# Weight decoding through a ring of three zeroed tiles, scaled copies that GpSimd may take, and an earlier start, in a bucketed attention with a feed-forward layer

## The chip, the cores and the metric

The kernel runs on one core of one Trainium2 chip. The metric is the device time of one execution in microseconds (us), as the median of the runs; lower is better.

## What is computed

The reference has two parts. The first is attention over 4 batches, 8 heads, 768 positions and 64 elements per head, in which a query sees only the keys of its own bucket (the signs of six projections). The second is a feed-forward layer on the attention's output, 3072 tokens by 512.

```python
q_bits = (np.einsum('bhsd,dk->bhsk', q, proj) > 0).astype(np.int64)
k_bits = (np.einsum('bhsd,dk->bhsk', k, proj) > 0).astype(np.int64)
...
mask = q_bucket[:, :, :, None] == k_bucket[:, :, None, :]
scores = scale * np.matmul(q, k.transpose(0, 1, 3, 2))
scores = np.where(mask, scores, -1000000000.0)
...
attn = np.exp(scores - max); attn = attn / (sum + 1e-09); x = attn @ v
h = x @ w_in
g = np.where(h > 0.0, h, alpha * (np.exp(np.minimum(h, 0.0)) - 1.0))
return (g @ w_out).astype(np.float32)
```

q, k, v and proj are float32; w_in (512 x 2048) and w_out (2048 x 512) arrive as float64.

## The kernel before

**Tiling.** Attention runs over 32 pairs of heads: 8 chunks (one batch and one half of its rows) of 4 pairs each. A pair has 6 row tiles of 128 queries, so there are 192 score tiles, numbered G = 0 to 191 (`pair_ops`). A float32 factor enters a matmul as two float16 halves, a high half (a scaled copy, written by `times`) and a low half (what the copy left over, written by `left_over`), and a product is three matmuls. For one score tile TensorE makes the scores (L896), VectorE takes them out of PSUM with the row maximum (L919) and makes the bias (`nb`, L936), ScalarE does the exponential (L947), VectorE the inverse sum (L985, L986), ScalarE or VectorE the high half (`hl`, through `times`, L356 or L358), VectorE the low half (L361), and a transposing DMA turns both for the product with V (L1076). The first four pairs (`whole`) skip the halves: TensorE turns their float32 tiles (`flip`, L963) and multiplies in float32 (L1046).

**Feed-forward.** `moe_ops` follows one chunk behind: matmuls into `h` (L1138), exponential and relu on ScalarE (L1162, L1166), their minimum on VectorE (L1169), two halves again (L356, L361), matmuls into `o` (L1190).

**Weights.** `weight_ops` loads 32 blocks of 128 x 512 float64 as pairs of 16-bit and 32-bit words, in staging places (`U`, three deep, and `raw`). For each block GpSimd zeroes the destination in `W` (L471, `zero`; from the fourth block on behind a one-element copy `tick`, L470, that makes GpSimd wait for an earlier block), ScalarE writes the top 16 bits of every element into it (L474, `top_`), and VectorE joins the low bits (L477, `join`). TensorE sums squares for a bound on all blocks (L489). After that `split` makes two float16 halves of each block in place of the float32 block in front of it: the high half by `hi` (operation `w{i}hi`, ScalarE or VectorE, L356 or L358), the low half by `lo` on VectorE (L361). Block i + 1 can be split only when block i has been, since its halves overwrite what block i was read from. `v_splits` makes the halves of V (`v{b}{p}hi` and `lo`), one operation of 128 x 768 per pair and batch.

**Order.** All operations are entered in a plan (`Plan.add`) with the engines that may run them ("AV" is ScalarE or VectorE), a cost, a due time and the operations they wait for. `Plan.order` then fixes the order on each engine: the first engine named takes the operation unless it would be busy for long and another is free earlier (`YIELD`). The instructions are issued in that order, engine by engine, and on the chip each engine works through its own list. SyncE (`S`) issues nearly all DMAs in one such list. In the first 32 us TensorE fills its gaps with `spin` matmuls (L1283) whose result nobody reads.

**Start.** `prep_ops` loads K and Q of a pair, scales them, makes halves, and turns them by transposing DMAs (`k_tr` L693, `q_tr` L724); K is duplicated (`k_dup`, L696), and bucket bits are computed from the turned tiles (`bits_ops`: matmuls L755, tests L763 or L776, and copies by DMA L785). `begin_ops` makes constants: GpSimd memsets, and the projection's halves (`rest_`, L412 to L419, all on VectorE). `v_ops` loads V (L803) and squares it on ScalarE (L352).

Of the kernel before, what the change touches and what calls it, by code (L numbers as in the profile page):

```python
# [7 lines left out]
F16 = mybir.dt.float16  # L8
# [20 lines left out]
DIRECT = 1  # L29
# [7 lines left out]
VD = -22  # L37
# [157 lines left out]

TINY = 160.0
# [3 lines left out]
def lsh_attention_moe(  # L200
# [38 lines left out]
    xp = ctx.enter_context(tc.tile_pool(name="xp", bufs=2))  # L239
# [9 lines left out]
        for name, cap in (  # L249
# [30 lines left out]

    ones = const.tile([P, P], BF16, name="ones")
# [14 lines left out]
    eye = W[:, NSI + 1, :P]  # L296
    area["ot"] = [W[:, NSI, :], W[:, NSI + NSO + 1, :]]
# [29 lines left out]
    def sum_over(mx, n):  # L327

        t = ps_a.tile([P, 512], F32, tag="av", name="sum")[:, :n]
        nc.tensor.matmul(t, ones, mx.bitcast(BF16).rearrange("p (n t) -> p n t", t=2)[:, :, 1], start=True, stop=True)  # L330
        return t
# [32 lines left out]
    def begin_ops():  # L364
# [35 lines left out]
        a = add("V", top_, TINY, -40, [loaded], name="pjx")  # L400
# [5 lines left out]
        b = add("P", sum_, 60.0, -40, [a, filled], new=[av], name="pjsum")  # L406

        def rest_():
            _, sc = exponents(pj["t"], 1, 2.0**-17, 13, "pj", small)
            hl = const.tile([P, 2, NB], F16, name="pjhl")  # L410
            pf, z = pj["f"], pj["z"]
            nc.vector.tensor_scalar(hl[:, 0], pf, sc, None, ALU.mult)  # L412
            nc.vector.scalar_tensor_tensor(hl[:, 1], pf, sc, hl[:, 0], ALU.mult, ALU.subtract)
            for n, (at, parts) in enumerate(
                ((1, ((0, P, 0),)), (1, ((0, P, 1),)), (0, ((0, D, 0), (D, P, 1))), (0, ((0, D, 1),)))
            ):
                for a_, z_, x in parts:
# [14 lines left out]
    def weight_ops():  # L432
# [887 lines left out]
```

## Time and profile before

| | |
|---|---|
| median of 3 runs | 858.01 us (857.25 to 860.03) |
| the profiled execution | 857.3 us, span 855.5 us from first to last instruction |
| TensorE busy | 816.5 us (95%), of it 21.9 us spin matmuls |
| ScalarE busy | 704.0 us (82%) |
| VectorE busy | 681.5 us (80%) |
| GpSimd busy | 22.9 us (3%), 15.9 us of it 32 memsets of weight blocks |

The profile names the engines PE (TensorE), DVE (VectorE), ACT (ScalarE), POOL (GpSimd) and SP (SyncE); PEld is TensorE's weight load. Busy shares over the whole span mix three stages: a start, a stretch in which scores of the first chunks and the weights' preparation lie together, and the long rest in which attention of one chunk and the feed-forward layer of the one before run side by side. A tile's name stands without its number, and `out<-in` is what an instruction writes and reads.

### The profile page before, as it was taken

How to read it: one execution, taken by the hardware profiler on the slowest of the kernel's cores; microseconds unless marked ns; L12 is line 12 of the kernel's file. 1: busy time of each engine (PE TensorE's matmuls, PEld its weight loads, DVE VectorE, ACT ScalarE, POOL GpSimd, SP SyncE). 2: the span in 40 equal slices, each digit the busy share in tenths (PEclk: the TensorE clock that was granted, in tenths of full speed). 3: DMA queues.
4: the chain of work that ended last, by engine and by line, in shares of the span. 5: the costliest groups of instructions: out<-in, count | busy, mean ns of one | idle time of the engine just before them, and what ended most of it. 6: DMA issues, size and time to landing. Idle time of an engine off the chain costs nothing. (4 is left out here: it accounts for less than half of the span.)

```text
span 855.5 us, 14970 instructions
## 1 busy us (share of the span) xinstructions
PE 816.5 (95%) x5298; PEld 439.5 (51%) x5301; DVE 681.5 (80%) x1520; ACT 704.0 (82%) x1292; POOL 22.9 (3%) x68
## 2 busy tenths in 40 slices
PE   8889869989999999999999999999999999999997
PEld 3455534444555555545555555555455555555553
DVE  6958999999998877888988778989888777773232
ACT  6679999999978889898888789888888878783543
POOL 3024000000000000000000000000000000000000
PEclk9989999999999999999999999999999999999999
DMA  9788767888989789958977888968877758571101
GB/s 283 141 237 288 267 128 127 150 190 146 152 165 178 126 179 224 183 111 152 181 147 135 138 190 187 216 98 157 167 143 140 131 105 158 98 105 38 38 1 37
DMA packets 367466, 128.99 MB, mean 151 GB/s; under 512 B 342248, under 2 KB 360352, under 8 KB 367392
## 3 DMA queue, kind: packets, MB, share of 16 engines
q1 hardware_dynamic: 367088, 127.91, 73.2%
q8 instruction: 41, 0.67, 0.3%
q14 instruction: 33, 0.27, 0.1%
q10 hardware_dynamic: 304, 0.13, 0.1%
HBM read 35.65 MB, written 6.29 MB: 49 GB/s over the span
## 5 line engine op out<-in xcount | busy, mean ns | idle before, releaser
L1138 PE MATMUL h<-x,W 128*128 128x384 f16 x1536 | 313.2, 327 | 7.8 <-ACT U L1166 7.2
L1190 PE MATMUL o<-W,U 128*128 128x512 f16 x1152 | 307.0, 379 | 2.4 <-ACT U L356 1.8
L947 ACT ACTIVATE pt<-pt,nb,sg 128x768 f32<-128x768 f32 x192 | 196.1, 1022 | 42.9 <-DVE nb L936 42.3
L1138 PEld LDWEIGHTS <-W 128*128 128x128 f16 x1536 | 148.8, 98 | 146.4 <-issue 15.5
L919 DVE TENSOR_SCALAR_CACHE_REDUCE pt<-s 128x768 f32<-128x768 f32 x180 | 171.5, 953 | 17.1 <-PE s L896 16.3
L361 DVE SCALAR_TENSOR_TENSOR hl<-pt,r,hl 128x768 f16<-128x768 f32 x168 | 165.1, 1013 | 7.9 <-ACT hl L356 7.4
L1190 PEld LDWEIGHTS <-U 128*128 128x128 f16 x1152 | 110.0, 97 | 105.6 <-issue 3.5
L896 PE MATMUL s<-K,O 128*128 128x384 f16 x720 | 147.8, 327 | 5.9 <-DVE pt L919 5.1
L356 ACT ACTIVATE hl<-pt,r 128x768 f16<-128x768 f32 x167 | 148.2, 929 | 1.8 <-DMA PT<-hl 0.6
L1169 DVE SCALAR_TENSOR_TENSOR U<-U 128x384 f32<-128x384 f32 x128 | 70.8, 553 | 52.5 <-ACT U L1166 52.2
L896 PEld LDWEIGHTS <-O 128*128 128x128 f16 (+1 forms) x768 | 73.2, 98 | 64.2 <-issue 19.6
L1162 ACT ACTIVATE U<-h,ch 128x384 f32<-128x384 f32 x128 | 73.1, 571 | 36.7 <-PE h L1138 36.5
L356 ACT ACTIVATE U<-U,sgg 128x384 f16<-128x384 f32 x128 | 78.1, 610 | 25.9 <-DVE U L1169 25.9
L361 DVE SCALAR_TENSOR_TENSOR U<-U,sgg 128x384 f16<-128x384 f32 x128 | 78.5, 614 | 22.2 <-ACT U L356 20.0
L1076 PE MATMUL av<-PT,vhl 128*64 128x384 f16 x1008 | 88.9, 327 | 3.1 <-DMA PT<-hl 3.1
L1076 PEld LDWEIGHTS <-vhl 128*64 128x64 f16 x1008 | 57.7, 110 | 33.3 <-issue 12.1
L1166 ACT ACTIVATE U<-h,ch 128x384 f32<-128x384 f32 x128 | 73.0, 571 | 0.0
L985 DVE TENSOR_SCALAR r<-sm 128x2 f32<-128x2 f32 x84 | 13.9, 165 | 31.4 <-ACT pt L947 30.9
L947 ACT ACTIVATION_READ_ACCUMULATOR pt<-pt,nb,sg 128x1 f32 x192 | 37.0, 193 | 0.0
L963 PE MATMUL flip<-W,pt 128*128 128x128 f32 x144 | 23.1, 286 | 3.8 <-ACT PT L356 2.7
L936 DVE TENSOR_SCALAR nb<-m,sg 128x2 f32<-128x2 f32 x96 | 23.4, 244 | 3.1
L1283 PE MATMUL spin<-ones 128*128 128x512 bf16 x81 | 21.9, 414 | 2.1 <-POOL ones L367 2.0
(126 smaller groups left out, 582.8 us busy)
## 6 DMA issues: line engine op xcount, KB each, us to landing
U<-in_moe_w_in_dram SPq DMA_DIRECT2D x12, 512.0 KB
vf<-in_v_dram SPq DMA_DIRECT2D x16, 384.0 KB
U<-in_moe_w_out_dram SPq DMA_DIRECT2D x12, 512.0 KB
qst<-in_q_dram SPq DMA_DIRECT2D x30, 192.0 KB
kst<-in_k_dram SPq DMA_DIRECT2D x14, 384.0 KB
out_dram<-W SPq DMA_DIRECT2D x16, 256.0 KB
PT<-hl SPq DMA_TRANSPOSE x168
W<-in_moe_w_in_dram SPq DMA_DIRECT2D x4, 512.0 KB
```

The source lines that it names most:

```text
L356: nc.scalar.activation(o, x, AF.Copy, scale=s)
L361: nc.vector.scalar_tensor_tensor(o, x, s, hi, ALU.mult, ALU.subtract)
L896: nc.tensor.matmul(s.t[:, y, :HALF], O[x][:rows, j * HC + t, :], K[x][:rows, j * NC + y * HC : j * NC + (y + 1) * HC, :].rearrange("p a b ...
L919: nc.vector.tensor_scalar(pt.t.rearrange("p (n e) -> p n e", n=2), s.t[:, :, :HALF], CLAMP, None, ALU.max, ALU.max, accum_out=m.t[:, y : y ...
L936: nc.vector.tensor_scalar(nb.t, m.t, sg_of(n), -1.0, ALU.mult, ALU.mult)
L947: nc.scalar.activation(pt_.t, pt_.t, AF.Exp, bias=nb.t[:, y : y + 1], scale=sg_of(n), accum_out=sm.t[:, z : z + 1])
L1076: nc.tensor.matmul(av.t[j * D : (j + 1) * D], vs["hl"][p].t[:, j, c, vx, :], PTs[j].t[:, :, px, c, :], start=y == 0, stop=y == 3 * NC - 1,)
L1138: nc.tensor.matmul(h.t, WH[:, g * KT + t, wx, fc * P : (fc + 1) * P], xbuf[NP * ci + t].t[:, xx, :], start=t == 0 and y == 0, stop=t == KT ...
L1162: nc.scalar.activation(e.t, h.t, AF.Exp, scale=c["ch"])
L1166: nc.scalar.activation(hp.t, h.t, AF.Relu, scale=c["ch"])
L1169: nc.vector.scalar_tensor_tensor(e.t, e.t, -1.0, hp.t, ALU.add, ALU.min)
L1190: nc.tensor.matmul(banks[t][:, :DO], g16.t[:, gx, t * P : (t + 1) * P], WH[:, NSI + 1 + f, wx, :], start=f == 0 and y == 0, stop=f == NF - ...
```

## The change

1. **Ring of zeroed tiles.** The 32 memsets of weight blocks and the 15 `tick` copies go. A tile `X` of 8 slots of 128 x 384 float32 takes the place of the pool `xp` (the attention's output halves); its upper four slots serve as three tiles of 128 x 512 (`tops`) that GpSimd zeroes once. ScalarE writes a block's top bits into one of the three (`top_`), and VectorE joins low bits and that tile into `W`. The outputs of later pairs wait for all joins before they use those slots (`topped`).
2. **GpSimd for scaled copies.** `w{i}hi` and `v{b}{p}hi` may run on "GAV", GpSimd first, at a planning cost of 0.9 n + 200 ns (`third`).
3. **The first pair is turned by TensorE.** K and Q of pair 0 go through 24 matmuls of 128 columns against a float16 unit matrix (`turned`) into score banks, and four copies of 128 x 768 bring them to SBUF; the two transposing DMAs of that pair go.
4. **Order.** V's first loads are due earlier (`VD` from -22 to -40), the projection's constants too; the copies of the projection's halves move from VectorE (10 instructions) to ScalarE (6); a sum of the first pairs uses another PSUM bank.

```diff
-VD = -22
+VD = -40
+GP = 0.9
+WH_ = ("GAV", "GAV")
...
+def third(n):
+    return (GP * n + 200.0, *either(n, pointer=True))
...
+    X = const.tile([P, 2 * NP, HALF], F32, name="X")
+    tops = X[:, NP:].rearrange("p a b -> p (a b)").rearrange("p (a b) -> p a b", b=SL)
...
-            nc.vector.tensor_scalar(o, x, s, None, ALU.mult)
+            (nc.gpsimd if e == "G" else nc.vector).tensor_scalar(o, x, s, None, ALU.mult)
...
-        c = add("V", rest_, 16 * 130.0, -30, [b, cleared], use=[av], name="pjz")
+        c = add("V", rest_, 6 * 140.0, -80, [b, cleared], use=[av], name="pjhl")
+        d = add("A", put, 6 * 130.0, -75, [c], name="pjz")
...
-            def zero():
-                if gate:
-                    nc.gpsimd.tensor_copy(tick, W[:1, places[i - 3], :1])
-                nc.gpsimd.memset(d, 0.0)
+            h = buf("top")
 
             def top_():
-                nc.scalar.activation(d.bitcast(F16).rearrange("p (n x) -> p n x", x=2)[:, :, 1], t.t["top"], AF.Copy)
+                h.t = tops[:, h.slot]
+                nc.scalar.activation(h.t.bitcast(F16).rearrange("p (n x) -> p n x", x=2)[:, :, 1], t.t["top"], AF.Copy)
 
             def join():
-                nc.vector.scalar_tensor_tensor(di, t.t["low"], 13, di, ALU.logical_shift_right, ALU.bitwise_or)
+                nc.vector.scalar_tensor_tensor(di, t.t["low"], 13, h.t.bitcast(I32), ALU.logical_shift_right, ALU.bitwise_or)
...
+        def zero():
+            nc.gpsimd.memset(X[:, NP:], 0.0)
...
-            a = add("AV", hi, either(SL, pointer=True), due, [decoded[i], maxes[o], *last.get(o, eye_users if o else [])], name=f"w{i}hi")
+            a = add(WH_[0], hi, third(SL) if len(WH_[0]) > 2 else either(SL, pointer=True), due, [decoded[i], maxes[o], *last.get(o, eye_users if o else [])], name=f"w{i}hi")
...
+    def turned(x, new, to, kept, nat, deps, due, name, nats=()):
...
+                for c in range(2 * HC):
+                    nc.tensor.matmul(
+                        s.t[:, c // HC, c % HC * P : (c % HC + 1) * P], x[:, 2 * HC * y + c, :], eye16, start=True, stop=True
+                    )
...
+                times(o, s.t[:, :, :HALF], e=e)
...
-            a = add("AV", hi, either(2 * NC * D, pointer=True), due, [st["scaled"]], after=pace, new=[hl], use=[f], name=f"v{b}{p}hi")
+            a = add(WH_[1], hi, third(2 * NC * D) if len(WH_[1]) > 2 else either(2 * NC * D, pointer=True), due, [st["scaled"]], after=pace, new=[hl], use=[f], name=f"v{b}{p}hi")
```

GpSimd (POOL), at the end of the constants of the start. Before, it then zeroes one block of `W` after the other, with a `tick` copy ahead of each (the last two rows begin that series):

```order
L378 MEMSET pjt 6x1 x4
L379 MEMSET W 128x128
L380 ISA
L380 AFFINE_SELECT W<-W 128x128
L471 MEMSET W 128x512
L470 COPY tick<-W 1x1
```

In the changed kernel (`vhl` is a pair of halves of V, `w0s` and `w1s` the scales of w_in and w_out):

```order
L387 MEMSET W 128x128
L388 AFFINE_SELECT W<-W 128x128
L366 TENSOR_SCALAR vhl<-vf,vs 128x12x64 x2
L366 TENSOR_SCALAR W<-W,w0s 128x512
L366 TENSOR_SCALAR vhl<-vf,vs 128x12x64 x2
L366 TENSOR_SCALAR W<-W,w0s 128x512 x6
L366 TENSOR_SCALAR W<-W,w1s 128x512
```

The 32 memsets and the copies have left the list, and all 32 high halves of weights and all 16 of V stand in it; none is left on the other two engines.

VectorE (DVE), where the weights' halves begin, around the 24th score tile (numbers tell the buffers apart). Before:

```order
L477 SCALAR_TENSOR_TENSOR W_93<-U_91,W_93 128x512
L358 TENSOR_SCALAR W_93<-W_93,w0s_1089 128x512
L361 SCALAR_TENSOR_TENSOR W_93<-W_93,w0s_1089 128x512
L477 SCALAR_TENSOR_TENSOR W_93<-W_93 128x512
L358 TENSOR_SCALAR vhl_1292<-vf_405,vs_739 128x12x64
L361 SCALAR_TENSOR_TENSOR vhl_1292<-vf_405,vs_739,vhl_1292 128x12x64
```

In the changed kernel:

```order
L369 SCALAR_TENSOR_TENSOR W_91<-W_91,w0s_1092 128x512
L489 SCALAR_TENSOR_TENSOR W_91<-W_91,X_89 128x512
L369 SCALAR_TENSOR_TENSOR vhl_1101<-vf_234,vs_483,vhl_1101 128x12x64
L489 SCALAR_TENSOR_TENSOR W_91<-U_88,X_89 128x512
L369 SCALAR_TENSOR_TENSOR W_91<-W_91,w0s_1092 128x512
L369 SCALAR_TENSOR_TENSOR vhl_1177<-vf_247,vs_483,vhl_1177 128x12x64
L1112 TENSOR_TENSOR xw_1295<-av_1215,xw_1295 128x384
L489 SCALAR_TENSOR_TENSOR W_91<-U_88,X_89 128x512
L369 SCALAR_TENSOR_TENSOR W_91<-W_91,w0s_1092 128x512
L1119 TENSOR_TENSOR X_89<-xw_1295,X_89 128x384
L369 SCALAR_TENSOR_TENSOR vhl_1194<-vf_260,vs_483,vhl_1194 128x12x64
```

The scaled copies (L358) are gone, and low halves and joins stand close together; each low half now needs a GpSimd result.

SyncE (SP), behind the first loads. Before:

```order
L454 DMA U<-in_moe_w_in_dram 128x2048
L724 DMA_TRANSPOSE O<-natq 128x12x128
L454 DMA U<-in_moe_w_in_dram 128x2048 x2
L693 DMA_TRANSPOSE K_243<-natk 128x12x128
L803 DMA vf<-in_v_dram 128x2x384
L693 DMA_TRANSPOSE K_293<-W 128x12x128
```

In the changed kernel:

```order
L470 DMA U<-in_moe_w_in_dram 128x2048
L859 DMA vf<-in_v_dram 128x2x384 x4
L470 DMA U<-in_moe_w_in_dram 128x2048 x2
L737 DMA_TRANSPOSE K_320<-W 128x12x128
L777 DMA_TRANSPOSE O<-W 128x12x128
L470 DMA W<-in_moe_w_in_dram 128x2048
```

All four loads of V now stand ahead of the second pair's transposes, and the first pair's two transposes are gone.

## Rows read from the trace of the kernel before

**Rows 1.** The page's first two parts: busy time, share and instructions of each engine; and tenths of busy time in 40 slices of 21.4 us.

```profile
PE 816.5 (95%) x5298; PEld 439.5 (51%) x5301; DVE 681.5 (80%) x1520; ACT 704.0 (82%) x1292; POOL 22.9 (3%) x68
...
PE   8889869989999999999999999999999999999997
...
DVE  6958999999998877888988778989888777773232
ACT  6679999999978889898888789888888878783543
```

**Rows 2.** Busy time by stretch: limits in us, length, then busy us of PE, PEld, DVE, ACT and POOL (instructions in brackets), TensorE's granted clock, DMA share, GB/s. The limits are the starts of VectorE's maxima of the score tiles 0, 24 and 60.

```profile
0.00:25.70 25.70, 21.92 (x116) 9.49 (x122) 18.23 (x63) 14.65 (x29) 7.68 (x32) 1.00 1.03 270
25.70:99.80 74.10, 64.01 (x476) 38.02 (x469) 59.70 (x142) 62.16 (x128) 13.77 (x33) 0.95 0.79 232
99.80:252.70 152.90, 137.60 (x907) 72.57 (x908) 147.28 (x327) 148.69 (x273) 1.48 (x3) 0.99 0.82 160
252.70:840.00 587.30, 582.09 (x3751) 314.47 (x3750) 452.73 (x986) 472.90 (x855) 0.00 (x0) 1.00 0.71 136
```

**Rows 3.** Groups by line and form: line, engine, operation, out<-in, form, count | busy us, mean ns | idle time before it and what ended it. The copies that the change moves, and the work that stays on VectorE.

```profile
L356 ACT ACTIVATE W<-W,w1s 128x512 f16<-128x512 f32 x16 | 11.5, 719 | 0.2 <-DVE W L361 0.2
L356 ACT ACTIVATE W<-W,w0s 128x512 f16<-128x512 f32 x13 | 9.4, 721 | 0.0
L356 ACT ACTIVATE vhl<-vf,vs 128x768 f16<-128x768 f32 x14 | 13.0, 933 | 0.0
L358 DVE TENSOR_SCALAR W<-W,w0s 128x512 f16<-128x512 f32 x3 | 1.4, 483 | 0.0
L358 DVE TENSOR_SCALAR vhl<-vf,vs 128x768 f16<-128x768 f32 x2 | 1.2, 613 | 0.0
L361 DVE SCALAR_TENSOR_TENSOR hl<-pt,r,hl 128x768 f16<-128x768 f32 x168 | 165.1, 1013 | 7.9 <-ACT hl L356 7.4
L361 DVE SCALAR_TENSOR_TENSOR U<-U,sgg 128x384 f16<-128x384 f32 x128 | 78.5, 614 | 22.2 <-ACT U L356 20.0
L1169 DVE SCALAR_TENSOR_TENSOR U<-U 128x384 f32<-128x384 f32 x128 | 70.8, 553 | 52.5 <-ACT U L1166 52.2
L919 DVE TENSOR_SCALAR_CACHE_REDUCE pt<-s 128x768 f32<-128x768 f32 x180 | 171.5, 953 | 17.1 <-PE s L896 16.3
L936 DVE TENSOR_SCALAR nb<-m,sg 128x2 f32<-128x2 f32 x96 | 23.4, 244 | 3.1
```

**Rows 4.** VectorE in order of time: start us, duration us, then as above; idle time before it in square brackets.

```profile
8.85 0.17 DVE L418 COPY pjz<-pjhl 128x6 f16<-128x6 f16 x1
...
9.78 1.00 DVE L361 SCALAR_TENSOR_TENSOR natk<-kst,qks,natk 128x768 f16<-128x768 f32 x1
...
20.27 1.18 DVE L696 COPY K<-K 64x1536 f16<-64x1536 f16 x1
...
25.24 0.54 DVE L696 COPY K<-K 64x1536 f16<-64x1536 f16 x1
...
54.50 1.32 DVE L477 SCALAR_TENSOR_TENSOR W<-U,W 128x512 int32<-128x512 int32 x2
...
79.16 1.39 DVE L936 TENSOR_SCALAR nb<-m,sg 128x2 f32<-128x2 f32 x1
79.28 1.26 DVE L919 TENSOR_SCALAR_CACHE_REDUCE pt<-s 128x768 f32<-128x768 f32 x1
```

**Rows 5.** GpSimd in order of time, the same columns.

```profile
4.50 0.21 POOL L379 MEMSET W<- 128x128 f32 x1
4.78 0.29 POOL L380 TENSOR_SCALAR_AFFINE_SELECT W<-W 128x128 f32<-128x128 f32 x1
...
13.81 0.18 POOL L470 COPY tick<-W 1x1 f32<-1x1 f32 x1 [8.26 <-DVE W L477]
...
20.33 0.52 POOL L471 MEMSET W<- 128x512 f32 x1
...
55.33 0.54 POOL L470 COPY tick<-W 1x1 f32<-1x1 f32 x1 [1.84 <-DVE W L477]
...
78.13 2.87 POOL L471 MEMSET W<- 128x512 f32 x6
```

**Rows 6.** Waits of VectorE between 25.7 and 99.8 us: who waited for whom, us in total, times, longest.

```profile
DVE W L477 <- ACT W L474: 5.7, 5, 1.9
DVE zb L776 <- PE z L755: 2.4, 1, 2.4
DVE pt L919 <- PE s L896: 2.1, 1, 2.1
```

**Rows 7.** What stands behind these waits, in order of time, TensorE, SyncE and ScalarE together: start us, duration us.

```profile
44.22 1.04 PE L755 MATMUL z<-O,pjz 128*32 128x384 f16 x6 [1.79 <-DMA O<-natq]
...
45.34 0.42 SPq L803 DMA_DIRECT2D vf<-in_v_dram  x1
...
51.86 0.82 ACT L352 ACTIVATE W<-vf 128x768 bf16<-128x768 f32 x1
```

**Rows 8.** Groups by line and form as in rows 3: the evictions, squares and spin matmuls that serve as prices for the start.

```profile
L356 ACT ACTIVATE PT<-flip 128x384 f32<-128x384 f32 x47 | 20.8, 485 | 2.9 <-PE av L1046 2.0 <-PE flip L963 0.7
L352 ACT ACTIVATE W<-vf 128x768 bf16<-128x768 f32 x4 | 3.3, 828 | 0.0
L1283 PE MATMUL spin<-ones 128*128 128x512 bf16 x81 | 21.9, 414 | 2.1 <-POOL ones L367 2.0
```

More of the change, by code (lines that the diff above doesn't have):

```diff
@@ L325, in scalar_in, with sum_over @@
         return small.tile(shape, F32, tag=tag, name=tag, **kw)
-    def sum_over(mx, n):
-        t = ps_a.tile([P, 512], F32, tag="av", name="sum")[:, :n]
+    def sum_over(mx, n, bank="av"):
+        t = (ps_h if bank == "h" else ps_a).tile([P, 512], F32, tag=bank, name="sum")[:, :n]
         nc.tensor.matmul(t, ones, mx.bitcast(BF16).rearrange("p (n t) -> p n t", t=2)[:, :, 1], start=True, stop=True)
@@ L382, in clear, with small_eye @@
             )
+        def small_eye():
+            nc.gpsimd.memset(eye16, 1.0)
+            nc.gpsimd.affine_select(
+                out=eye16, in_=eye16, compare_op=ALU.is_equal, fill=0.0, base=0, pattern=[[-1, P]], channel_multiplier=1
+            )
         filled = add("G", one, 150.0, -60, name="ones")
+        squared = add("G", small_eye, 500.0, -55, name="eye16")
         cleared = add("G", clear, 3000.0, -50, name="clear")
@@ L439, in one @@
             place = i + 1 + o
-            places.append(place)
             raw = i % 4 == 0 and (place + 1) * SL <= RAW
@@ L552, in slot_after, with turn, evict @@
         return [scored[x]] if x >= 0 and x in scored else []
+    def turned(x, new, to, kept, nat, deps, due, name, nats=()):
+        evs = []
+        for y in range(2):
+            s = buf("so" if y else "s")
+            def turn(y=y, s=s):
+                pool, tag = (ps_o, "o") if y else (ps_s, "s")
+                s.t = pool.tile([P, 2, 512], F32, tag=tag, name="so" if y else "s")
+                for c in range(2 * HC):
+                    nc.tensor.matmul(
+                        s.t[:, c // HC, c % HC * P : (c % HC + 1) * P], x[:, 2 * HC * y + c, :], eye16, start=True, stop=True
+                    )
+            def evict(e, y=y, s=s):
+                if y == 0:
+                    new()
+                o = to()[:, 2 * HC * y : 2 * HC * (y + 1), :].rearrange("p (a c) e -> p a (c e)", a=2)
+                times(o, s.t[:, :, :HALF], e=e)
+            tr = add("P", turn, 6 * 56.0, due, [*deps, squared], new=[s], use=[nat, *nats], late=160.0, name=name)
+            ev = add(
+                "AV", evict, either(S, True), due, [tr], after=evs[:1], new=[] if y else [kept], use=[s, kept] if y else [s],
+                name=name + "ev",
+            )
+            evs.append(ev)
+        return evs
     def prep_ops(ns):
@@ L586, in load_k @@
                     )
-                i["kl"] = track(add("S", load_k, 460.0, begin[n] - 17 - lead, after=after, new=[i["kb"]], late=1000.0, name=f"k{n}load"))
+                i["kl"] = track(add("S", load_k, 460.0, begin[n] - 17 - lead, after=after, new=[i["kb"]], late=2600.0 if n == 1 else 1000.0, name=f"k{n}load"))
             i["qb"] = buf("qst" + own)
```

87 lines of the change are left out of this document (49 added, 38 removed), and 1 row of the table rings.

## The prediction, made before the changed kernel ran

> **What bounds the kernel now.** I read the page's busy shares first, then its 40 slices, then busy time by stretch, then rows in order of time. The shares name TensorE, busy 95% [rows 1]; the slices show where that holds. From the tenth slice on TensorE is at 9 nearly throughout, before that not, and there VectorE and ScalarE stand at 8 or 9 [rows 1]. So I cut the span at three of VectorE's own instructions, the maxima of score tiles 0, 24 and 60 [rows 2]. From tile 60 (252.7 us) to 840 us TensorE is busy 582.1 of 587.3 us, VectorE 452.7 and ScalarE 472.9: TensorE sets the pace, and a part of a microsecond more or less on the others disappears. From tile 24 to tile 60 VectorE is busy 147.3 of 152.9 us and ScalarE 148.7, while TensorE has 15.3 us idle: here VectorE, and ScalarE about as much, set when TensorE gets its next tile. From tile 0 to tile 24 nobody is full (VectorE 59.7 and ScalarE 62.2 of 74.1 us): waits. Up to tile 0, 25.7 us, VectorE works 18.2 us.
>
> From this follows the form of the sum. The feed-forward layer's place in TensorE's list at tile 60 is the same in both kernels, so what matters is **when VectorE reaches the maximum of tile 60**; from there on TensorE carries any shift to the end. VectorE's 252.7 us until then are 18.2 + 59.7 + 147.3 = 225.2 us of work and 27.5 us of waits (7.5 + 14.4 + 5.6) [rows 2]. I change these two sums.
>
> **Work that VectorE loses.** Three high halves of weights by 0.48 us and two of V by 0.61 us are 2.7 us [rows 3]. Ten tiny copies of the projection's halves, which fill VectorE from 8.85 to 9.78 us, are 0.9 us [rows 4]. Third, the 32 memsets that go were not free: VectorE's duplicate of K took 1.18 us at 20.27 and 0.54 us at 25.24; during the first, GpSimd ran a memset from 20.33 for 0.52 us [rows 4, 5]. A bias of 0.24 us in the mean took 1.39 us at 79.16, within a series of six memsets [rows 3 to 5]; the maximum beside it ended 0.3 us late. From such pairs I take 2 us in all for the memsets' hold on VectorE (bounds 1, as the K copy and the maximum show together, and 4). Against that stand two scaled copies and evictions more that fall to it, about 1 us. Sum: **-4.6 us**, rounded to -4.5.
>
> **What ScalarE loses.** 16 + 13 high halves of weights by 0.72 us are 20.9 us, and 14 of V by 0.93 us are 13.0 us, of which two fall into the first batch [rows 3]. It gains six tiny copies and four evictions of 768 columns, each bounded by one eviction of 384 (0.49 us) and two (0.97 us); with 0.85 us that is 3.4 us [rows 8]. The net loss of some 19 us before tile 60 does **not** shorten the path by itself, since VectorE's mandatory work is as long as the stretch. It can only take away VectorE's waits for ScalarE.
>
> **Waits.** Until tile 0: two transposing DMAs are replaced by 24 matmuls of TensorE, which until then only spins (21.9 us of spin matmuls hide them [rows 8]), but K's duplicate on VectorE now waits for two evictions behind ScalarE's other work, and three squares of V (0.83 us each [rows 8]) plus the four evictions and the tiny copies stand ahead of the first exponential. VectorE also takes the second pair's tests before its first maximum. I put 3 us more wait here: between 0 (all lies in the 7.5 us that it waits now) and 6 (the three squares and the four evictions, 5.9 us, one behind the other). Tile 0 to 24: the test that waited 2.4 us for TensorE and the maximum that waited 2.1 us [rows 6] hang on Q's late transpose at 44.2 us, behind bulk loads, and a load of V issued at 45.34 us whose square ran at 51.86 us, after which a join waited [rows 7]. With V's four loads first in SyncE's list and the first pair out of the transposes, these go, and about a third of the 5.7 us that joins wait for ScalarE [rows 6] as well; with the small ones I take 14.4 to 6.4, **-8 us** (bounds 0 and -11). Tile 24 to 60: 5.6 to 4.6, -1 us. Sum of waits: **-6 us** (3 - 8 - 1).
>
> **What GpSimd's copies cost VectorE.** No row has a scaled copy on GpSimd. The nearest rows: a memset of 128 x 512 takes 0.52 us and one of 128 x 128 takes 0.21; an affine select of 128 x 128, which reads and writes, takes 0.29 [rows 5]. Scaled by 0.29 / 0.21 the long one would be 0.71 us, and that I take; the ends are 0.52 and four selects, 1.16 us. GpSimd has room for it: 36 operations by 0.71 us are 26 us in over 150 us. But they hinder VectorE if the two exclude each other. Rows for that: GpSimd's one-element copy takes 0.18 us at 13.81 and 0.54 us at 55.33, where it ends with the second of VectorE's two joins (54.50 + 1.32) [rows 4, 5]; a join reads two operands from SBUF. So GpSimd's reading waits for such an instruction. That VectorE's two-operand instructions wait for a long GpSimd read is the other direction, and no row has it; the memsets show that direction only for one-operand copies. Bounds per operation: 0, and its whole length 0.71 us.
>
> The Trainium skill (SBUF — State Buffer, section "Who interferes with whom") says that a VectorE instruction with two SBUF inputs contends with a GpSimd instruction that reads SBUF, that whichever starts first has the shared ports for the whole instruction, and that the other blocks fully. By that rule every collision would be paid whole; how many there are it does not say.
>
> I count them by order. A high half on GpSimd is released when VectorE ends the low half before it. If VectorE then has a two-operand instruction, GpSimd waits and gets in behind it, and the instruction after that is blocked if it too has two operands; if VectorE has a maximum (0.95 us, from PSUM [rows 3]), GpSimd's copy lies beside it. The three commonest two-operand groups are 314 of VectorE's 681 us, 46% [rows 1, 3]; joins and low halves of weights, which fill the list here, raise that to some 60%. 0.6 x 0.6 x 0.71 us is 0.26 us, and with now and then a low half waiting for its high half 0.3 us: 36 operations (32 blocks, the first batch's V) make **+10.8 us**.
>
> **The sum.** -4.5 - 6 + 10.8 = +0.3 us: the profiled execution's 857.3 us become 857.6. It lies 0.7 us under the median of the runs, so in their terms 858.3; I say **858 us, no change that can be measured** (0.3%, 2.6 us, is about the least that shows). Beyond tile 60 twelve copies of V move from ScalarE to GpSimd at no price: TensorE covers both engines there.
>
> **Rivals.**
> 1. *GpSimd's copies do not hold VectorE up* (its two-operand instructions win, or GpSimd slips in between). For it: the direction that would cost is in no row, and what the memsets hold up are copies and small scalings with one operand. Against it: the one-element copy's waits. Then the third term falls to 0 to 3 us: 858 - 10.8 = 847 us, to 850. Chance 0.28.
> 2. *VectorE is blocked whole, slower.* The place is tile 24 to 60, where VectorE has 5.6 us to spare. In the piece of its list shown for the changed kernel 10 of 11 instructions read two SBUF operands, so nearly every copy there collides; then each low half waits for a high half that waited. At 0.55 us for each of 36 operations the term is 20 us, at 0.71 us 26: 867 to 873 us. It decides from 0.4 us per operation on (+3.6 us over the sum's value, 862). The rule quoted above is the reason to give it weight. Chance 0.20.
> 3. *The start costs more than it gives.* V's four loads ahead of the second pair's transposes, and V's squares ahead of the first exponential: the first maximum comes 6 us later instead of 3, and the waits of tiles 0 to 24 fall by 4 instead of 8: +7, 865 us. Chance 0.10.
>
> That the change does not reach the engines is excluded: all 48 copies stand in GpSimd's list. What the freed ScalarE time could do more is in rival 1's lower end: if VectorE's waits fell by 11 us instead of 6, the sum would be 853.
>
> **How the numbers follow.** The forecast case, 0.42, spans 852 to 864 (per-operation price 0.15 to 0.45 us). Split by the 2.6 us bound: a third faster, two fifths even, the rest slower. Faster: 0.28 + 0.14 = 0.42. Slower: 0.20 + 0.10 + 0.08, less the mild ends of both rivals that stay within the bound, 0.36. Even: 0.22. For 8 in 10 I take 846 to 868: rival 1 whole and the lower half of rival 2; its own range is 852 to 864.
>
> **What would show it.** Right: high halves on POOL of 0.6 to 0.8 us, some twice that where they waited; the joins (now L489), 0.66 us each in the pair at 54.50 [rows 4], and the weights' low halves (now L369) some 0.1 to 0.3 us longer in the mean; the first maximum at 28 to 30 us, tile 24 near 98, tile 60 near 253; ScalarE with idle time before tile 60, VectorE without. Wrong: low halves as short as before and tile 60 near 242 (rival 1), or VectorE's joins at 1.3 us and low halves behind POOL for over 15 us in all (rival 2), or tile 24 after 103 us (rival 3). A second stall of TensorE on ScalarE's evictions past tile 60 would break the premise that a shift is carried unchanged to the end.

## The result, and the profile after

The changed kernel takes **866.5 us** (median of four runs, 865.67 to 867.3), the kernel before 858.01 us on the same chip: ratio 1.0087, interval [1.0062, 1.0112]. It got slower by 0.9%, where no measurable change was forecast; the time lies above the forecast case (852 to 864 us) and inside the range for 8 in 10 (846 to 868). One run of e2, further down, took 958.41 us at a granted clock of 0.84, where its other three had 0.98, and is left out of e2's time. The profiled execution took 866.8 us, its span 865.1 us against 855.5 us.

The page's first two parts, of the changed kernel (as [rows 1]):

```profile
PE 820.8 (95%) x5322; PEld 441.9 (51%) x5322; DVE 687.3 (79%) x1506; ACT 680.7 (79%) x1258; POOL 107.6 (12%) x72
...
PE   8898876989999999989999999999999999999997
...
DVE  5878899999997978889987878889987877773232
ACT  7689859867897989887887889888888878784543
POOL 2202773445000000022000000031000000000000
```

The load went where the change sends it: ScalarE lost 23 us, GpSimd gained 85, and it is at 2 to 7 tenths from the fourth to the tenth slice. VectorE, which was to lose copies and to be held up, is 5.8 us longer busy. TensorE's span is longer by 9.6 us: 4.3 us of more busy time (820.8 against 816.5) and 5.3 us of more idle time (44.3 against 39.0).

Busy time by stretch, cut again at the maxima of score tiles 0, 24 and 60 (as [rows 2]; limits in us, length, busy us of PE, PEld, DVE, ACT and POOL, TensorE's granted clock, DMA share, GB/s):

```profile
0.00:28.78 28.78, 24.98 (x154) 11.04 (x154) 19.06 (x57) 22.76 (x48) 4.75 (x24) 1.00 0.96 273
28.78:109.81 81.03, 70.04 (x527) 43.99 (x527) 66.36 (x162) 67.21 (x138) 27.89 (x12) 0.94 0.71 211
109.81:259.60 149.79, 133.17 (x847) 68.25 (x844) 142.18 (x299) 119.09 (x216) 54.52 (x29) 0.97 0.72 143
259.60:840.00 580.40, 572.16 (x3696) 308.61 (x3695) 453.31 (x981) 461.71 (x838) 20.40 (x8) 1.00 0.72 140
```

Tile 60 comes at 259.6 us instead of 252.7. Until then VectorE worked 227.6 us (19.1 + 66.4 + 142.2; 225.2 before) and waited 32.0 us (9.7 + 14.7 + 7.6; 27.5 before). The prediction had 225.2 - 4.5 + 10.8 = 231.5 us of work and 27.5 - 6 = 21.5 us of waits, 253.0 in all. So the work came out 3.9 us under the forecast, the waits 10.5 us over it.

Groups by line and form in the changed kernel (columns as in [rows 3]); L366 is the scaled copy on VectorE or GpSimd, L369 the low half, L489 the join:

```profile
L366 POOL TENSOR_SCALAR vhl<-vf,vs 128x768 f16<-128x768 f32 x16 | 40.7, 2547 | 387.1 <-DVE vs L355 185.5 <-DMA K<-zb 171.5 <-ACT U L364 10.6
L366 POOL TENSOR_SCALAR W<-W,w0s 128x512 f16<-128x512 f32 x16 | 33.1, 2069 | 55.2 <-PE s L952 45.4 <-DVE W L369 9.7
L366 POOL TENSOR_SCALAR W<-W,w1s 128x512 f16<-128x512 f32 x16 | 29.1, 1820 | 39.8 <-DVE W L369 35.1 <-DVE r L1041 4.3 <-PE rows L1092 0.3
...
L489 DVE SCALAR_TENSOR_TENSOR W<-U,X 128x512 int32<-128x512 int32 x24 | 16.9, 710 | 6.7 <-ACT X L486 6.7
...
L369 DVE SCALAR_TENSOR_TENSOR W<-W,w0s 128x512 f16<-128x512 f32 x16 | 13.1, 821 | 5.7 <-POOL W L366 5.7
L369 DVE SCALAR_TENSOR_TENSOR W<-W,w1s 128x512 f16<-128x512 f32 x16 | 12.3, 768 | 1.2 <-POOL W L366 1.2
```

The low halves of weights in the kernel before (L361):

```profile
L361 DVE SCALAR_TENSOR_TENSOR W<-W,w0s 128x512 f16<-128x512 f32 x16 | 11.9, 746 | 0.8 <-ACT W L356 0.7
L361 DVE SCALAR_TENSOR_TENSOR W<-W,w1s 128x512 f16<-128x512 f32 x16 | 11.9, 745 | 0.1
```

**GpSimd's copy takes 1.8 to 2.5 us in the mean**, not 0.71, and VectorE's low halves wait for it. Its waits between 28.8 and 260 us (columns as in [rows 6]):

```profile
DVE W L489 <- ACT X L486: 8.4, 9, 2.6
DVE W L369 <- POOL W L366: 6.9, 9, 1.5
```

The first blocks of weights show the mechanism. GpSimd, then VectorE, in order of time (start us, duration us, idle time before in brackets):

```profile
99.75 2.27 POOL L366 TENSOR_SCALAR W<-W,w0s 128x512 f16<-128x512 f32 x1 [0.88 <-DVE W L369]
102.89 2.65 POOL L366 TENSOR_SCALAR W<-W,w0s 128x512 f16<-128x512 f32 x1 [0.88 <-DVE W L369]
106.43 1.56 POOL L366 TENSOR_SCALAR W<-W,w0s 128x512 f16<-128x512 f32 x1 [0.88 <-DVE W L369]
```
```profile
100.97 0.71 DVE L489 SCALAR_TENSOR_TENSOR W<-U,X 128x512 int32<-128x512 int32 x1
102.05 0.75 DVE L369 SCALAR_TENSOR_TENSOR W<-W,w0s 128x512 f16<-128x512 f32 x1 [0.37 <-POOL W L366]
102.72 0.55 DVE L1119 TENSOR_TENSOR X<-xw,X 128x384 f16<-128x384 f32 x1
103.19 1.01 DVE L369 SCALAR_TENSOR_TENSOR vhl<-vf,vs,vhl 128x768 f16<-128x768 f32 x1
104.11 0.61 DVE L832 TENSOR_SCALAR zb<-z,pjt 128x384 f16<-128x384 f32 x1
104.64 0.68 DVE L489 SCALAR_TENSOR_TENSOR W<-U,X 128x512 int32<-128x512 int32 x1
105.58 0.75 DVE L369 SCALAR_TENSOR_TENSOR W<-W,w0s 128x512 f16<-128x512 f32 x1 [0.26 <-POOL W L366]
```

A block goes round in 3.1 to 3.5 us: 2.27 or 2.65 us of copy, 0.03 us later the low half of 0.75 us, and 0.09 us after its end GpSimd starts again (102.89 against 102.05 + 0.75). The 0.88 us in GpSimd's brackets is its whole idle time between two copies, so nearly all of it is that low half. Since block i + 1 may be split only after block i, the copy's length stands in this chain in full; VectorE waited for GpSimd at 9 of the 32 low halves.

TensorE waits in turn. Its waits for VectorE's next maximum between 28 and 260 us, before and in the changed kernel (columns as in [rows 6]):

```profile
PE s L896 <- DVE pt L919: 4.3, 7, 1.2
PE s L952 <- DVE pt L975: 15.0, 14, 2.4
```

Other waits became shorter, those for ScalarE in the feed-forward layer above all, so that TensorE's idle time up to tile 60 is 31.4 us against 29.2; its busy time is 228.2 us against 223.5. A part of that is a lower granted clock. Four stretches of the changed kernel, columns as above:

```profile
95.00:98.00 3.00, 1.53 (x18) 1.05 (x16) 2.76 (x4) 2.78 (x6) 2.12 (x2) 1.00 1.14 291
98.00:102.00 4.00, 3.39 (x19) 2.52 (x20) 3.31 (x5) 2.46 (x5) 3.12 (x2) 0.61 0.52 98
...
128.00:132.00 4.00, 2.56 (x17) 1.41 (x16) 3.93 (x10) 3.87 (x8) 1.18 (x1) 1.00 1.10 227
132.00:140.00 8.00, 4.98 (x15) 1.94 (x14) 7.69 (x17) 7.97 (x14) 1.56 (x1) 0.57 1.13 228
```

Before each fall TensorE stood idle for a good part: it was busy 1.53 of 3 us and 2.56 of 4 us at full clock. In the stretch behind it the mean granted clock is 0.61 or 0.57, which is mostly the lower level, 1.2 GHz. The mean granted clock over the span is 0.987 against 0.993, that is 22 us at 1.2 GHz against 12 (the missing share of the span, doubled); half of the 10 us more would be 5 us of matmul time, an estimate that fits the 4.3 us that TensorE is longer busy. The clock alone does not make the time: the runs of g3 below have 0.983 to 0.990, those of the changed kernel 0.987 to 0.989, and g3 takes 860.94 us.

### The profile page after: what moved, and what is told of

The parts are those of the page before. It is cut to its first block, busy times and chain, and to the rows that moved or that the text cites. A ratio compares the mean times of both kernels' runs of the same rounds, so it can differ in the third digit from the quotient of the medians.

```text
span 865.1 us, 14994 instructions
## 1 busy us (share of the span) xinstructions
PE 820.8 (95%) x5322; PEld 441.9 (51%) x5322; DVE 687.3 (79%) x1506; ACT 680.7 (79%) x1258; POOL 107.6 (12%) x72
## 5 line engine op out<-in xcount | busy, mean ns | idle before, releaser
L1198 PE MATMUL h<-X,W 128*128 128x384 f16 x1536 | 310.5, 326 | 0.1
L369 DVE SCALAR_TENSOR_TENSOR hl<-pt,r,hl 128x768 f16<-128x768 f32 x168 | 167.3, 1025 | 7.3 <-ACT hl L364 7.1
L369 DVE SCALAR_TENSOR_TENSOR U<-U,sgg 128x384 f16<-128x384 f32 x128 | 79.0, 617 | 20.4 <-ACT U L364 18.5
L366 POOL TENSOR_SCALAR vhl<-vf,vs 128x768 f16<-128x768 f32 x16 | 40.7, 2547 | 387.1 <-DVE vs L355 185.5
L366 POOL TENSOR_SCALAR W<-W,w0s 128x512 f16<-128x512 f32 x16 | 33.1, 2069 | 55.2 <-PE s L952 45.4
L1041 DVE TENSOR_SCALAR r<-sm 128x2 f32<-128x2 f32 x84 | 15.9, 190 | 27.6 <-ACT pt L1003 27.4
L366 POOL TENSOR_SCALAR W<-W,w1s 128x512 f16<-128x512 f32 x16 | 29.1, 1820 | 39.8 <-DVE W L369 35.1
```

What stands on the lines that cost most here:

```text
L366: (nc.gpsimd if e == "G" else nc.vector).tensor_scalar(o, x, s, None, ALU.mult)
L369: nc.vector.scalar_tensor_tensor(o, x, s, hi, ALU.mult, ALU.subtract)
L1198: nc.tensor.matmul(h.t, WH[:, g * KT + t, wx, fc * P : (fc + 1) * P], xbuf[NP * ci + t].t[:, xx, :], start=t == 0 and y == 0, stop=t == KT ...
```

## The experiments

Two theories stood at first: A, GpSimd's copies cost the time; B, the new start and order do. The next runs split theory A: L, the copies hold VectorE's instructions up at shared memory ports; W, VectorE and TensorE wait for slow copies. The last ones set W against R, the other order that the planner makes when GpSimd is in its list. All ratios are to the kernel before, run beside them on the same chip. Starts of VectorE's maximum in us, each column from one profiled execution, which the text below uses:

| tile | before | changed | e3 | f1 | f3 | f4 | g1 | g2 | h1 |
|---|---|---|---|---|---|---|---|---|---|
| 24 | 99.8 | 109.8 | 103.9 | 103.2 | 112.8 | 108.2 | 108.1 | 102.6 | 107.5 |
| 60 | 252.7 | 259.6 | 248.9 | 248.1 | 256.3 | 261.1 | 263.1 | 247.1 | 260.1 |
| 84 | 341.5 | 346.9 | 345.0 | 341.8 | 349.4 | 348.4 | 356.2 | 340.6 | 347.1 |
| 96 | 390.2 | 398.8 | 393.7 | 390.4 | 399.4 | 399.1 | 405.3 | 389.9 | 396.8 |

The runs of one kernel lie up to 10 us apart (before: 854.87 to 864.78), and the profiled one of e3 is 3.3 us above its median, that of h1 3.4 below, so a difference of 3 us between columns says little. Nor is tile 60 the same place in every order. When its maximum started, TensorE had begun 255 `h` and 172 `o` matmuls in the kernel before and 258 and 174 in the changed one, but 246 and 165 in e3, f1 and g2, 247 and 165 in g1, 243 and 161 in f3, 261 and 176 in f4 and h1. At tile 84 it is 435 and 307 in all of the table: that row compares equal work.

**e3: the change without GpSimd's copies.**

```diff
-WH_ = ("GAV", "GAV")
+WH_ = ("AV", "AV")
```

> The changed kernel with the high halves planned for ScalarE and VectorE as before; ring of zeroed tiles, TensorE's turn of the first pair and the early loads of V stay. Theory A: 850 to 857 us, under the kernel before by what the start gives. Theory B: 863 us or more.

857.41 us, ratio 0.999 [0.9956, 1.0024], 0.4 us above theory A's range. Ring, start and earlier loads together give nothing that can be measured. Letting GpSimd into the list turns this kernel into the changed one: 9 us.

**e2: the kernel before, with GpSimd in the list of its copies alone** (`third` and the two lists).

```diff
+GP = 0.9
+WH_ = ("GAV", "GAV")
...
-            a = add("AV", hi, either(SL, pointer=True), due, [decoded[i], maxes[o], *last.get(o, eye_users if o else [])], name=f"w{i}hi")
+            a = add(WH_[0], hi, third(SL), due, [decoded[i], maxes[o], *last.get(o, eye_users if o else [])], name=f"w{i}hi")
...
```

> The kernel before with one part of the change alone: high halves of weights and V may run on GpSimd at the same planning cost; zeroing, start and transposes stay as they were. Theory A: 864 to 872 us. Theory B: 855 to 860 us.

876.77 us, ratio 1.0207 [1.0171, 1.0243]: slower on the old start and with the old memsets too, 5 us beyond what theory A had. With e3 it says that the loss comes with GpSimd in the copies' list and not with the rest of the change. Whether it is GpSimd's time or the order that the planner then makes, neither tells.

**e1: order of the change, the 48 copies issued on ScalarE at the same places.**

```diff
-            o.run(o.eng) if len(o.engs) > 1 else o.run()
+            o.run("A" if o.eng == "G" else o.eng) if len(o.engs) > 1 else o.run()
```

> The changed kernel's plan, order and waits are kept; only the engine is another: the 48 high halves that the plan gives to GpSimd are issued on ScalarE at the same place. Theory A (GpSimd's copies cost the time: 1.56 and 2.20 us each instead of 0.71, they hold up two-operand instructions on VectorE and low halves wait for them; 7 us of lengthening and 7 us of waits before tile 60): 853 to 858 us. Theory B (the new start and the new order of the lists cost it, GpSimd's copies lie beside other work): 864 to 867 us, as the changed kernel.

870.16 us, ratio 1.0137 [1.0104, 1.0169]. Both theories missed: taking GpSimd out of this order makes it slower still. ScalarE has 48 copies more at places that the planner chose for another engine, and VectorE's joins wait 13.4 us for it until tile 60 (8.4 in the changed kernel). So its time does not tell the theories apart. But it measures the lengthening: until tile 60 VectorE runs the same 515 instructions in both. From the start to that maximum, e1 and then the changed kernel (columns as in [rows 2]):

```profile
0.00:267.60 267.60, 229.40 (x1524) 122.80 (x1525) 222.84 (x515) 233.30 (x442) 4.76 (x24) 0.96 0.72 173
0.00:259.60 259.60, 228.18 (x1524) 123.28 (x1525) 227.59 (x515) 209.06 (x402) 87.16 (x64) 0.96 0.74 179
```

GpSimd's copies make VectorE's work 4.8 us longer (227.59 against 222.84), and no single instruction by more than 0.53 us.

**e4: the planner told 2.5 ns an element instead of 0.9.**

```diff
-GP = 0.9
+GP = 2.5
...
-    return (GP * n + 200.0, *either(n, pointer=True))
+    return (GP * n + 280.0, *either(n, pointer=True))
```

> The changed kernel with GpSimd's planning cost at what its trace shows (2.5 n + 280 ns: 1.56 us for 512 columns, 2.20 us for 768) instead of 0.9 n + 200, so that the plan gives GpSimd fewer copies and places low halves later. Theory A: 854 to 862 us, between the changed kernel and the one without GpSimd. Theory B: 863 us or more.

866.01 us, ratio 1.0084 [1.0052, 1.0116]. That is theory B's range, but no evidence for it: GpSimd still got 47 of the 48 copies, since it stands first in the list and is hardly ever busy, so the edit did not do what it was made for. The low halves waited 3.6 us for GpSimd here, 6.9 in the changed kernel, and the time is the same within the noise, which speaks against the wait alone.

**f1: e3, and as much work on GpSimd that nobody waits for** (scaled copies of finished data in pieces of 128 columns, three for a block, four for a V).

```diff
+                for n in range(3):
+                    nc.gpsimd.tensor_scalar(idle, W[:, d, n * P : (n + 1) * P], wst["sc", o], None, ALU.mult)
...
+                for n in range(4):
+                    nc.gpsimd.tensor_scalar(idle, done[:, n * P : (n + 1) * P], st["sc"], None, ALU.mult)
```

> The change with its scaled copies planned for VectorE and ScalarE alone (857.4 us), and behind every low half GpSimd makes scaled copies of finished data into a tile that nobody reads: three of 128x128 for each of the 32 weight blocks and four for each of the 16 pairs of V, so that GpSimd is busy about as long as in the change and nobody waits for it. Theory L (GpSimd's copies hold VectorE's instructions up at the memory they share): 861 to 868 us, VectorE's low halves, tops and joins longer than 0.75 us on average. Theory W (the time goes into VectorE's and TensorE's waits for the slow GpSimd copies): 856 to 860 us.

859.9 us, ratio 1.0008 [0.9985, 1.0031]: under L's range and in W's. GpSimd was busy 146.2 us, more than in the change, and the low halves of weights took 0.762 and 0.763 us (e3: 0.746 and 0.744); that is over L's mark of 0.75, but by 2% only. Until tile 60 VectorE worked 3.3 us longer than in e3 (222.8 against 219.5). The tile view of f1 has shortest, median and longest time in ns:

```profile
L914 POOL TENSOR_SCALAR idle<-vhl,vs x64: 602/657/2210, 69.7 to 615.4; 128x128 f16<-128x128 f32 x64
L549 POOL TENSOR_SCALAR idle<-W,w0s x48: 602/832/2677, 75.3 to 176.6; 128x128 f16<-128x128 f32 x48
L549 POOL TENSOR_SCALAR idle<-W,w1s x48: 602/700/2089, 113.8 to 200.0; 128x128 f16<-128x128 f32 x48
```

The one that suffers is GpSimd: 0.60 us at its shortest, up to 2.68 us beside VectorE. The longest, and VectorE at that time (L370 is f1's low half, L1235 the minimum in the feed-forward layer):

```profile
141.64 2.68 POOL L549 TENSOR_SCALAR idle<-W,w0s 128x128 f16<-128x128 f32 x1
```
```profile
141.53 1.93 DVE L370 SCALAR_TENSOR_TENSOR hl<-pt,r,hl 128x768 f16<-128x768 f32 x2
143.38 0.55 DVE L1235 SCALAR_TENSOR_TENSOR U<-U 128x384 f32<-128x384 f32 x1
```

Three two-operand instructions ran through meanwhile, at their usual length (two of 1.0 us, which overlap a little, and one of 0.55). These pieces are shorter than the change's copies, though, so one hold is shorter too: in the changed kernel the longest low half of a weight took 1.17 us, here 0.86. f1 shows that GpSimd's time as such costs nothing that can be measured; it does not show that long copies hold VectorE as little.

**f3: only the weights' copies on GpSimd; f2: the same, but GpSimd hardly reads.** First the edit of both, then what f2 has besides:

```diff
-WH_ = ("GAV", "GAV")
+WH_ = ("GAV", "AV")
```
```diff
+                if e == "G":
+                    nc.gpsimd.memset(WH[:, d, 0, :], 0.0)
+                    for n in range(4):
+                        times(WH[:, d, 0, 8 * n : 8 * n + 8], W[:, d + 1, 8 * n : 8 * n + 8], wst["sc", o], e)
```

> Only the weights' high halves may run on GpSimd, V's on VectorE and ScalarE. By the trace of the change, 5.4 of its 8.6 us are there by tile 84, before the second batch of V: 862 to 865 us with either theory. If V's later copies are what costs, 857 to 860.

> V's copies on VectorE and ScalarE; a weight block's high half on GpSimd is a memset of 128x512 and four scaled copies of 8 columns each, so GpSimd takes about as long (some 1.6 us) and the low half still waits for it, but GpSimd reads nearly nothing (the high halves hold zeros, so this output is not the reference's). Compare with the run that has only the weights' real copies on GpSimd. Theory L: 2 us or more below that run, 856 to 861 us. Theory W: as that run, within 1.5 us.

f3: 868.13 us, ratio 1.0105 [1.0069, 1.0142], 3 us over the expectation. f2: 869.2 us, ratio 1.0112 [1.0077, 1.0148]. The reads are gone, and so is the lengthening, but not the time. The stand-in is longer than what it stands for, 2.16 us of GpSimd for a block against 1.88 (GpSimd's busy time, 74.0 and 64.8 us, less the 4.8 us of its other work, over 32). Low halves of f3, then of f2:

```profile
L369 DVE SCALAR_TENSOR_TENSOR W<-W,w0s 128x512 f16<-128x512 f32 x16 | 12.9, 809 | 10.7 <-POOL W L366 10.6
L369 DVE SCALAR_TENSOR_TENSOR W<-W,w1s 128x512 f16<-128x512 f32 x16 | 12.3, 770 | 0.9 <-POOL W L366 0.9
```
```profile
L369 DVE SCALAR_TENSOR_TENSOR W<-W,w0s 128x512 f16<-128x512 f32 x16 | 12.0, 750 | 11.3 <-POOL W L366 11.3
L369 DVE SCALAR_TENSOR_TENSOR W<-W,w1s 128x512 f16<-128x512 f32 x16 | 11.9, 742 | 2.9 <-POOL W L366 2.9
```

VectorE's busy time is 3.4 us shorter in f2 (678.0 against 681.4), its wait for GpSimd 2.7 us longer. The longer stand-in can account for that: 10 low halves waited in f3 and 13 in f2, by 0.28 us each some 3 us (an estimate). So L does not make f3's 9 us, but some 3 of them may be the lengthening; the wait, 11.5 us in f3, is the larger part.

**f4: only V's copies on GpSimd.**

```diff
-WH_ = ("GAV", "GAV")
+WH_ = ("AV", "GAV")
```

> Only V's high halves may run on GpSimd (16 copies), the weights' on VectorE and ScalarE. The prediction held that V's 12 later copies cost nothing: 857 to 859 us. By the trace of the change, where 3 to 5 us come between tiles 84 and 144 with the second and third batch of V: 860 to 863.

864.65 us, ratio 1.0065 [1.0045, 1.0084], above both expectations: GpSimd in V's list alone costs, against the prediction. But most of the loss is not in V's later batches: tile 84 is 6.9 us behind the kernel before, tile 96 8.9. Nor does VectorE wait for GpSimd before them: its low halves of V wait 1.3 us in the whole run, after 380 us.

**g1 and g2: order and start of e3, with all 48 copies (g1) or V's 16 (g2) issued on GpSimd at their places.**

```diff
-            o.run(o.eng) if len(o.engs) > 1 else o.run()
+            copy = o.name.endswith("hi") and o.name[0] in "wv"
+            o.run("G" if copy else o.eng) if len(o.engs) > 1 else o.run()
```

In g2 the test is `o.name[0] == "v"`.

> Order and start of the run without GpSimd's copies (857.4 us), but at the places where that order has them, all 48 scaled copies are issued on GpSimd. It differs from the run with idle copies only in that low halves now wait for GpSimd. Theory W (waiting for the slow copies costs): 865 us or more, low halves waiting over 8 us for GpSimd up to tile 60. Theory R (the waiting is cheap and the other order that the planner chooses with GpSimd in its list costs the 9 us): 856 to 861.

> The same order, only V's 16 high halves on GpSimd. Theory W: 859 to 863 us, with waits of VectorE's vhl low halves for GpSimd in each batch. Theory R: 857 to 859, so that the 864.7 us of V's copies with the planner's own order come from that order.

g1: 873.23 us, ratio 1.0169 [1.0148, 1.019]. g2: 859.68 us, ratio 1.001 [0.9993, 1.0027]. So at e3's places V's copies cost nothing that can be measured, though 859.68 lies in theory W's range by its letter (the kernel before took 859.32 beside it, and the low halves of V waited 1.3 us in all), and the weights' cost 13.5 us. g1 and f1 have the same order; in g1 somebody waits. In g1 the score tile itself stands behind it, VectorE in order of time:

```profile
104.30 0.75 DVE L369 SCALAR_TENSOR_TENSOR W<-W,w0s 128x512 f16<-128x512 f32 x1 [1.76 <-POOL W L366]
106.82 1.38 DVE L369 SCALAR_TENSOR_TENSOR W<-W,w0s 128x512 f16<-128x512 f32 x1 [1.76 <-POOL W L366]
108.13 0.94 DVE L975 TENSOR_SCALAR_CACHE_REDUCE pt<-s 128x768 f32<-128x768 f32 x1
```

The maximum of tile 24 at 108.13 is the instruction that TensorE needs for its next scores; in f1 it starts at 103.2. Until tile 60 g1 loses 15.0 us to f1, 10.3 in VectorE's waits (35.6 against 25.3; 8.4 of g1's are for GpSimd) and 4.7 in its work, and at the end of the span 16.4. The 4.7 are more than they seem: f1 has seven scaled copies of weights on VectorE, 3.3 us, that g1 has not, so g1's other instructions are 8.0 us longer. The two runs differ in who waits and also in the length of a copy, so this pair shows what the weights' copies cost at these places, not the wait by itself.

**h1: order of f4, V's copies issued on ScalarE.** (The edit of e1, with the lists of f4.)

```diff
-WH_ = ("GAV", "GAV")
+WH_ = ("AV", "GAV")
...
-            o.run(o.eng) if len(o.engs) > 1 else o.run()
+            o.run("A" if o.eng == "G" else o.eng) if len(o.engs) > 1 else o.run()
```

> The order that the planner makes when only V's copies may run on GpSimd (864.7 us there), with these 16 copies issued on ScalarE at the same places (0.93 us each instead of 2.2 to 3.3). Theory R (this order itself costs 5 us, for it hands six more of the weights' first copies to ScalarE and VectorE waits for each): 862 to 867 us. Theory W (GpSimd's length costs there too): 857 to 860.

865.64 us, ratio 1.0074 [1.005, 1.0098]: as f4 within 2.5 us at each tile of the table, without GpSimd. That is R's range. By itself it has e1's weakness, since ScalarE gets 16 copies at places planned without them; but f4's own trace has no wait for GpSimd before 380 us, and g2 costs nothing, so for V it is R, the order. The planner, whose ScalarE is free of V, hands 15 of the 16 first weight copies to ScalarE (9 in e3), and VectorE's low halves of weights wait for ScalarE four times until tile 60, 3.5 us in all (2.8 in f4, 0.6 in e3). Those of `w_in`, e3 first, then h1:

```profile
L369 DVE SCALAR_TENSOR_TENSOR W<-W,w0s 128x512 f16<-128x512 f32 x16 | 11.9, 746 | 0.8 <-ACT W L364 0.6
```
```profile
L369 DVE SCALAR_TENSOR_TENSOR W<-W,w0s 128x512 f16<-128x512 f32 x16 | 11.9, 746 | 2.3 <-ACT W L364 2.3
```

The joins wait longer for ScalarE as well, 7.7 us against 5.0. Between 85 and 115 us VectorE is busy 29.09 us in e3 and 22.59 in h1, and TensorE's mean granted clock there is 1.00 in e3 and 0.83 in h1. The hand-overs are a part of this; what else in that order makes the rest was not taken apart.

**g3: GpSimd as last choice.**

```diff
-WH_ = ("GAV", "GAV")
+WH_ = ("AVG", "AVG")
...
-    return (GP * n + 200.0, *either(n, pointer=True))
+    return (*either(n, pointer=True), GP * n + 1100.0)
```

(with GP = 2.5.)

> GpSimd as last choice instead of first, planned at 2.5 ns an element and 1.1 us of hand-over: the planner gives it 19 of the 48 copies, where ScalarE and VectorE are both behind. Theory W: between the run without GpSimd and the change, 859 to 863 us. Theory R: anywhere from 857 to 866, not in proportion to the number of copies. A version that beats the kernel before would show here below 856.

860.94 us, ratio 1.0019 [1.0002, 1.0036]. GpSimd took 22 copies, not 19 (14 of weights, 8 of V), and no low half shows a wait for it. The time is in the ranges of both theories and does not tell them apart. No wait, little loss; but no gain either. No run beat the kernel before.

## Why the prediction was wrong

**Forecast and result.** No measurable change was forecast; the time rose by 8.5 us (0.9%), out of the forecast case, to which 0.42 was given, and within the range for 8 in 10. The result lies just under where rival 2 ended (867 to 873), but not by its price. By the sum's own terms tile 60 was to come at 253.0 us and came at 259.6: the work was 3.9 us under the forecast, the waits 10.5 over it.

- **The step that failed: the length of GpSimd's copy, and with it a wait that had no term.** I scaled a select against a memset [rows 5] to 0.71 us, with 1.16 as upper end. Undisturbed it takes 1.56 us for 128 x 512 (many rows read exactly so), 2.20 for 128 x 768, and 1.8 to 2.5 in the mean. Both ends were too low. From that came the second fault: I gave **the low halves' wait for GpSimd** no term of its own, only "now and then". It is 6.9 us to tile 60; with 0.71 us a copy I took it for next to nothing: in the trace of before the weights' low halves waited 0.9 us in all, behind copies of 0.72 us on ScalarE [rows 3].
- **Waits, -6 us.** Measured +4.5 (27.5 to 32.0). 6.9 of it is GpSimd; without that the waits would be 25.1, a gain of 2.4. The joins' waits for ScalarE grew instead of shrinking by a third: 8.4 us, where 5.7 [rows 6] was to become 3.8. These two, 6.9 and 4.6 us over it, make up the 10.5 us that the waits lie over the forecast, and 1 us more. The second does not need GpSimd, since the joins wait 7.0 us in e3 too. Of the other parts, the start's +3 was near (7.5 to 9.7 us; the maximum of tile 0 at 28.8 us, forecast 28 to 30). The 2.4 us for the test are gone as forecast, but with the joins and 2.4 us for GpSimd in their place tiles 0 to 24 wait 14.7 us, not 6.4 (14.4 before).
- **VectorE's hold, +10.8 us.** Right in kind, less than half in size: 4.8 us by e1, 0.13 us for each of 36 operations where 0.3 was said. The saved work was too high as well, since the total is +2.4 and so the rest -2.4, where -4.5 was said; the two errors cancel in part. The hold is a part of the loss, but not what the forecast missed. The Trainium skill (SBUF — State Buffer, section "Who interferes with whom") has the ports as an exclusive lock under which the later instruction blocks fully. The runs show most of the loss on GpSimd's side (f1: 0.60 to 2.68 us, with VectorE's two-operand instructions going past at their usual length), and on VectorE never a whole copy: 0.53 us at most in the change.
- **Rival 1** (GpSimd does not hold VectorE) was near on the mechanism, but its 847 to 850 us was wrong even so: e3, without any copy on GpSimd, gains nothing. **Rival 2** had "each low half waits for a high half that waited". That wait is real, and the weights' copies do stretch, to 3.1 us at most; VectorE blocked whole is not (joins 0.71 us, not 1.3). **Rival 3**'s sign, tile 24 after 103 us, came (109.8), but e3 passes it too (103.9) and loses nothing. TensorE had done more by tile 24, 144 turning matmuls (`flip`) against 120, so that sign was no good measure.
- **From tile 60 on TensorE carries the shift.** Half right, and here the form of the sum is weak. The change is 6.9 us behind at tile 60, 5.4 at tile 84 and 9.6 at the end; g1 against f1 carries it (15.0 and 16.4). But e3 is 3.8 us ahead at tile 60 and 3.5 behind at tile 84, f3 3.6 behind and then 7.9. The premise that the feed-forward layer stands at the same place in TensorE's list held for the change, but not for them: e3 had 9 `h` and 7 `o` matmuls fewer behind it, f3 12 and 11. So the maximum of tile 60 is a fair mark only where the order agrees, and tile 84 is a better one. The change also loses another 3.2 us between tiles 84 and 96, where V's second batch is. The order alone does not do that: e1, with the change's order and V's copies on ScalarE, takes 49.3 us there (before 48.7, changed 51.9), and g2, with these copies on GpSimd at e3's places, 49.3 as well. By these single executions it takes both together.
- **V's later copies at no price**: right in g2, where they keep their places; the planner's new order is what costs in f4.
- **The chances.** A third and two fifths of 0.42 leave 0.11 for the slower part, not the 0.08 in the sum for "slower"; its total of 0.36 comes out with 0.11, less 0.05 for the mild ends.

What stays open: how the change's 8.5 us divide among the wait, the lengthening and the order. f3's 9.2 and f4's 5.7 us do not add up to them, since each list of engines makes another order; e4 halved the wait and gained nothing clear; and a run with the change's own order, full-length copies on GpSimd and nobody waiting is missing. Open is also whether the clock's share is only a consequence of TensorE's waits: the mean clock of f1's runs is 0.989 to 0.998, of g1's 0.984 to 0.986.

## What to carry to other kernels

When work moves to a slower engine, price first the instruction that waits for it on the engine that sets the pace, with the slower engine's whole length in that chain, before asking whether the two engines disturb each other; in these runs the idle engine was cheap only for results that nobody needed soon. Where the trace has no row for an operation, a memset is no price for a converting copy: the bound from above must allow several times as much (here three times the memset: 1.56 us against 0.52). And a planner that is given one more engine makes another order, so the order has to be held still (issue at the same places) before the engine is blamed, and two orders are compared at a point where every engine has done the same work. Idle time in the brackets of a row reaches back to the engine's own last instruction; it is not the time from the releaser to the start.

## What the runs showed of the hardware

- A scaled copy from float32 to float16 on GpSimd takes 1.56 us for 128 x 512 and 2.20 us for 128 x 768, 2.5 ns for each further element of a row; back to back, such copies of 128 x 512 start 1.53 to 1.54 us apart (113.46, 115.00 and 116.53 us in the changed kernel). VectorE does the former in 0.48 us and ScalarE in 0.72. The Trainium skill (GPSIMD Engine Reference, section "4.1 Engine selection") calls one-input work on GpSimd roughly line-rate; this copy, with one tile and a scale for each row as inputs, takes three times as long as on VectorE.
- A copy of 128 x 8 took 0.30 us in f2 at its shortest and 0.42 to 0.44 in the mean, a memset of 128 x 512 0.52 us: neither the start of an instruction nor the writing makes up the 1.56 us.
- Beside a busy VectorE, GpSimd's short copy stretches to some four times its length at most (f1: 0.60 to 2.68 us), while VectorE's low halves grow by 1 to 3% in the mean (1.022 us against 1.014 for the large low half of the attention, 0.763 against 0.744 for the weights'). Beside full-length copies the weights' first low halves grow by 10% (0.821 us in the change, 0.746 in e3).
- The hand-over is short: GpSimd started 0.09 to 0.17 us after the end of the low half that released it, and the low half 0.03 to 0.04 us after the end of the copy that it waited for (changed kernel, f3 and g1).
